# Batch selection in an attention and expert kernel: the first gather ahead of weight rounding, two gate dot products on other engines, score rows of four batches by way of DRAM

## Chip, cores and metric

One core of a Trainium2 chip. The metric is the device time of one execution in microseconds; the kernel before was run three times: 250.52 us median, 248.71 lowest, 251.86 highest. Engines: PE (TensorE), DVE (VectorE), ACT (ScalarE), POOL (GpSimd), SP (SyncE, which here only issues DMAs).

## What is computed

Attention in a sliding window of 64 over 8 batches, 8 heads, 576 positions, head size 64; then, per batch, the 128 rows with the highest gate score go through a two-layer expert and are added back.

```python
scores = scale * q @ k.T; scores = where(0 <= i - j < 64, scores, -1e9)
x = softmax(scores) @ v                      # per batch (576, 512)
s = x @ w_gate                               # gate score of each row
top = argpartition(-s, 128)[:128]            # per batch
out = x
out[top] = x[top] + sigmoid(s[top])[:, None] * (relu(x[top] @ w1) @ w2)   # 512 -> 1024 -> 512
```

All arithmetic that decides is fp32; the expert's operands are split into a rounded high part and a rest, and three products are summed.

## The kernel before

The 72 windows are worked in 36 pairs, called tiles m here (128 rows each; a batch is 4.5 tiles). The main loop at the end of the function has slots n = 0 to 38, and a tile passes through three of them: scores, maxima and exponentials in slot m, transposes of the probabilities in slot m+1, the product with V (av), the normalisation into x and the gate score in slot m+2. The order in which the loop calls the steps is the order of instructions on every engine; each engine works its own list in order. Loads for tile n+2 are issued at the head of slot n on SP, together with one or two 256 KB pieces of the expert weights (the table PIECES) and the stores of finished tiles; pool sizes hold SP back, so that it runs at most some two slots ahead of the engines.

Attention by engine and slot: PE does 32 score matmuls (s), 64 av matmuls and 8 transposes (t). DVE does 8 masked maxima (attn_max, line 270, each followed by a read of its accumulator), a reciprocal, the normalisation (line 322) and the gate (gate_dot, line 230: product with w_gate and sum, 128x512). ACT does 8 exponentials in two halves (line 278), two copies of transposed probabilities (pt) and the sums (z, line 314).

The weight pieces are rounded on POOL (split_w, lines 198 to 203), two instructions each, in the slot after the load: the high part (line 200) and the rest (line 202). Eight pieces are w1 (steps 0 to 7), eight are w2.

A batch is chosen by a generator, choose(b), started in the slot in which the gate scores of its first four tiles are there. It yields the name of the place in the loop at which it wants to go on: R, F, S at the head of a slot, P behind the scores, F0 behind P, R0 behind av, S0, V at the end behind the gate, E behind the expert's share of the slot. Its steps: the gate scores of five tiles, each a column of 128 values, are spread on PE to rows in PSUM, the same on all 128 partitions, by transposes of a broadcast column (spread, line 423), four in one step and the fifth in another; ACT copies them to the tile row (line 430); DVE compares every score with every other (compare, line 439) in steps of two tiles; PE sums the comparisons (lo, line 471); DVE forms the rank and the selection (sel, lines 477 to 487; for most batches the selection is on POOL); PE turns it into row numbers (ix, line 498); DVE makes integers of them (fx, idx, lines 502 and 504); and a DMA on POOL's queue gathers the chosen rows from DRAM (xe, line 506). Batches 0 and 7 are urgent and compare in two parts; batch 0 compares straight from PSUM. For batches 0 and 1 the steps stand at P, R0, S0, F0, for the others at E, R, S, F.

The expert is a second generator (moe). It takes a gathered batch from the slot after its gather on: four transposes of xe (xt, line 528), the split into high part (ACT, line 219) and rest (DVE, line 220), then nine quanta of matmuls at the end of every slot. From slot 12 on it fills PE, and after the last tile it goes on alone.

## Time and profile before

| | |
|---|---|
| median of 3 runs | 250.52 us (248.71 to 251.86) |
| the profiled execution, its own time | 249.5 us |
| its span in the profile | 247.8 us |
| PE busy | 92% |
| DVE busy | 74% |
| ACT busy | 63% |
| POOL busy | 29% |
| mean granted PE clock | 0.991 |

Shares are of the span. The chain of work that ended last runs through the expert's last products and the last scatter; the attention is over at about 190 us, and from there PE works on the expert alone. A share over the whole span is an average over these stages, so the rows below are of single stretches. Busy time of PE includes the overlap of pipelined matmuls. "issue" as the end of an idle time means that the profile shows nothing that was waited for.

### The profile page before, as it was taken

Reading aid. Unit: us, or ns where it says so; the run is one execution under the profiler, and the core shown is the slowest. Engines: PE = TensorE matmul, PEld = TensorE weight load, DVE = VectorE, ACT = ScalarE, POOL = GpSimd, SP = SyncE. Lnnn points to the kernel's source line nnn. Section 1 sums busy time; section 2 is a strip of 40 time slices with the busy share of each in tenths; the row PEclk is TensorE's granted clock in tenths of the full one; section 3 lists DMA queues with packets and bytes.
Section 4 is the critical chain, followed back from the end, with each engine's and each line's share of the span. In section 5 each row is a group of like instructions: output and inputs, shape, how many; then the busy total and the mean of one; then the engine's idle time right before and its main releaser. Section 6 shows DMA issues by size and latency. Waiting matters only on the chain. (4 is left out here: it accounts for less than half of the span.)

```text
span 247.8 us, 10898 instructions
## 1 busy us (share of the span) xinstructions
PE 228.5 (92%) x4406; PEld 198.4 (80%) x4406; DVE 182.5 (74%) x935; ACT 155.4 (63%) x457; POOL 71.1 (29%) x115
## 2 busy tenths in 40 slices
PE   8886787988898999999899999999999899999991
PEld 7675676777787888988788978888888899899891
DVE  0588899778888889879986898798879995342510
ACT  2997876786776986876878768859878122022100
POOL 7406783492640101014016010530061111110011
PEclk9999998899999999999999999999999999999999
DMA  6999998799566766866877672587212221101011
GB/s 231 389 385 376 329 357 263 252 309 356 183 173 177 218 229 194 276 199 188 256 235 236 189 233 91 168 288 246 74 46 87 109 65 44 42 3 42 0 45 42
DMA packets 25154, 47.26 MB, mean 191 GB/s; under 512 B 2960, under 2 KB 3984, under 8 KB 25104
## 3 DMA queue, kind: packets, MB, share of 16 engines
q1 hardware_dynamic: 23680, 42.10, 51.5%
q0 software_dynamic: 1280, 4.20, 5.3%
q8 instruction: 35, 0.57, 1.0%
q10 hardware_dynamic: 144, 0.26, 0.3%
q14 instruction: 15, 0.12, 0.1%
HBM read 35.01 MB, written 11.53 MB: 188 GB/s over the span
## 5 line engine op out<-in xcount | busy, mean ns | idle before, releaser
L278 ACT ACTIVATE p<-p,nm 128x128 f32<-128x128 f32 x288 | 91.8, 394 | 35.4 <-DVE nm L270 33.0
L270 DVE CUSTOM_DVE_ANT_0 p<-s,mask 128x128 f32<-128x128 f32 x288 | 63.5, 285 | 14.8 <-PE s L258 14.7
L304 PE MATMUL av<-v,pt 64*64 64x65 f32 x2176 | 42.1, 220 | 5.8 <-issue 5.8
L304 PEld LDWEIGHTS av<-v,pt 64*64 64x64 f32 x2176 | 39.1, 134 | 7.4 <-issue 6.3
L258 PE MATMUL s<-k,q 64*64 64x128 f32 x1152 | 41.8, 279 | 2.0 <-DVE nm L270 1.0
L286 PE MATMUL t<-ident,p 128*128 128x128 f32 x288 | 41.0, 284 | 0.9 <-DVE fx L502 0.6
L288 ACT COPY pt<-t 128x512 f32<-128x512 f32 x72 | 38.4, 580 | 3.9 <-PE t L286 3.1
L258 PEld LDWEIGHTS s<-k,q 64*64 64x64 f32 x1152 | 32.5, 135 | 10.2 <-issue 8.3
L286 PEld LDWEIGHTS t<-ident,p 128*128 128x128 f32 x288 | 31.5, 142 | 4.7 <-DVE fx L502 1.3
L230 DVE CUSTOM_DVE_ANT_0 jk<-x,wgb 128x512 bf16<-128x512 f32 x36 | 28.7, 797 | 1.2
L666 PE MATMUL yp<-w2h,hh 128*128 128x512 f32 (+1 forms) x72 | 27.8, 386 | 0.0
L322 DVE TENSOR_TENSOR x<-av,z 128x512 f32<-128x512 f32 x36 | 24.9, 692 | 3.4
L676 POOL DMA_INDIRECT out_dram<-xe,idx x8 | 8.1, 1009 | 67.1 <-DVE xe L671 32.4
L666 PE MATMUL yp<-w2l,hh 128*128 128x512 f32 (+1 forms) x72 | 26.9, 374 | 0.0
L666 PE MATMUL yp<-w2h,hl 128*128 128x512 f32 (+1 forms) x72 | 26.9, 373 | 0.0
L270 DVE DVE_READ_ACCUMULATOR2_ANT nm<- 128x1 f32 x288 | 23.6, 82 | 0.0
L439 DVE SCALAR_TENSOR_TENSOR cmp<-row,scores,later 128x128 bf16<-128x128 f32 (+11 forms) x39 | 19.9, 540 | 0.7 <-ACT row L430 0.5
L506 POOL DMA_INDIRECT xe<-out_dram,idx x8 | 8.3, 1040 | 39.9 <-DVE nm L270 29.5
L487 POOL TENSOR_SCALAR sel<-slots,diff 128x128 bf16<-128x128 f32 x16 | 11.7, 741 | 26.8 <-DVE diff L480 26.4
L625 PE MATMUL hp<-xh,w1h 128*128 128x256 f32 x64 | 18.4, 287 | 0.0
L625 PE MATMUL hp<-xl,w1h 128*128 128x256 f32 x64 | 18.2, 285 | 0.0
L625 PE MATMUL hp<-xh,w1l 128*128 128x256 f32 x64 | 18.1, 282 | 0.0
(88 smaller groups left out, 328.2 us busy)
## 6 DMA issues: line engine op xcount, KB each, us to landing
v<-in_v SPq DMA_DIRECT2D x36, 260.0 KB, 5.1
q<-in_q SPq DMA_DIRECT2D x36, 256.0 KB, 4.7
out_dram<-x SPq DMA_DIRECT2D x32, 256.0 KB, 3.9
k<-in_k SPq DMA_DIRECT2D x31, 256.0 KB, 4.8
st<-in_w SPq DMA_DIRECT2D x16, 256.0 KB, 4.1
k<-in_k SPq DMA_DIRECT2D x8, 128.0 KB
out_dram<-x SPq DMA_DIRECT2D x8, 128.0 KB, 2.7
k<-in_k ACTq DMA_DIRECT2D x1, 256.0 KB
```

The lines of the kernel that those rows point to most:

```text
L230: nc.vector.tensor_tensor_reduce(out=junk()[:n, :E], in0=xf[:n], in1=wgb[:n], op0=ALU.mult, op1=ALU.add, scale=1.0, scalar=0.0, accum_out=acc)
L258: nc.tensor.matmul(s[r][c * W:(c + 1) * W, j], Q[m][rs, j, c], keys(m, c, j, rs), start=True, stop=True)
L270: nc.vector.tensor_tensor_reduce(out=pe[:, j, :, r], in0=s[r][:, j], in1=mk, op0=ALU.add, op1=ALU.min, scale=-SCALE, scalar=3.0e38, accum_ ...
L278: nc.scalar.activation(pe[:, j, :, r], pe[:, j, :, r], AF.Exp, bias=nm[:, r, j:j + 1], scale=-1.0)
L286: nc.tensor.transpose(t[:, j, :], pe[:, j, a].rearrange("p r w -> p (r w)"), ident)
L288: nc.scalar.copy(pt, t)
L304: nc.tensor.matmul(av[cs, r, j * D1:(j + 1) * D1], pt[a][rs, j, cs], V[g // 2][rs, g % 2, j], start=a == 0 or o == c, stop=a == 1)
L322: nc.vector.tensor_tensor(out=x.rearrange("p j r d -> p r j d"), in0=av[:, :, :, :D], in1=z[:, 1].unsqueeze(3).to_broadcast([P, 2, NP, D]) ...
L439: nc.vector.scalar_tensor_tensor(out=above[t][r, c0:c1], in0=src[r, c0 - base:c1 - base], scalar=scores[r, m:m + 1], in1=later[r, c0 - a:c ...
L487: (nc.vector if urgent or b in (1, 6) else nc.gpsimd).tensor_scalar(out=sel[r], in0=slots[r], scalar1=diff[r, t:t + 1], scalar2=float(lo - ...
L625: nc.tensor.matmul(hp[:, j], w[:, c, js], a[:, c].rearrange("p u c -> p (u c)"), start=(n == 0), stop=(n == 3 * KC1 - 1))
L666: nc.tensor.matmul(yp[:C, :wide], a[:, c % per, us], w[:, c, es], start=(n == 0), stop=(n == 3 * KC2 - 1))
```

## The change

Six edits.

- Rows through DRAM, for batches 2 to 5: in place of five broadcast transposes, one transpose of the 128x5 block of scores (rt, 5 rows of 128), a small copy on ACT (rs), a DMA of 2.5 KB to a line in DRAM and a second DMA that reads this line to all 128 partitions of the tile row. It starts at P of the slot after the fifth tile's score, and the compares stay in their slots.
- Two gates lent: for tiles 5 and 6 POOL forms the product x * w_gate (prod) and ACT sums it with an accumulating activation, in the next slot. Both run behind other steps of that slot (flush).
- The first gather in front of rounding: the rounding of weight pieces moves from the head of a slot to behind F0, and so behind the first gather on POOL. PIECES loads each piece up to a slot earlier.
- lo of batch 0 moves from P to R0, behind the av matmuls.
- The first row copy of batch 1 and its transposes move to the end of slot 10 and the head of slot 11.
- The subtraction of the first split (batch 0, slot 10) moves behind the next slot's maxima on DVE (EARLY, behind_max).

```diff
 from contextlib import ExitStack
+from functools import partial
 
 import numpy as np
 
@@ -26,6 +27,9 @@
 
 URGENT = (0, 7)
 
+
+BY_DMA = (2, 3, 4, 5)
+
 GROUPS = ((0,), (1,), (2,), (3,), (4, 5), (6, 7))
 
 WARM = 8
@@ -34,7 +38,12 @@
 
 
 
-PIECES = {3: 1, 4: 1, 5: 1, 6: 2, 7: 2, 8: 1} | {n: 2 for n in range(9, 13)}
+PIECES = {2: 1, 3: 1, 4: 1, 5: 2, 6: 1, 7: 1, 8: 2, 9: 2, 10: 2, 11: 2, 12: 1}
+
+
+LENT = (5, 6)
+
+EARLY = 10
 
 CMPS = 2
 
@@ -217,8 +226,17 @@
         for c in range(0, n, step):
             r = slice(c, c + step)
             nc.scalar.copy(hi[:, r], ps[:, r])
-            nc.vector.tensor_tensor(out=lo[:, r], in0=ps[:, r], in1=hi[:, r].bitcast(F32),
-                                    op=ALU.subtract)
+            rest = partial(nc.vector.tensor_tensor, out=lo[:, r], in0=ps[:, r],
+                           in1=hi[:, r].bitcast(F32), op=ALU.subtract)
+            if slot <= EARLY:
+
+                behind_max.append(rest)
+            else:
+                rest()
+
+    behind_max = []
+    behind_exp = []
+    behind_gather = []
 
 
     def junk():
@@ -335,7 +353,19 @@
             nc.sync.dma_start(outs[b + 1][:W, :], xf[W:])
 
     def attn_gate(m):
-        gate_dot(st_x[m], scores[:, m:m + 1])
+        if m not in LENT:
+            gate_dot(st_x[m], scores[:, m:m + 1])
+            return
+        prod = p_h.tile([P, E], F32, tag="h", name=f"prod{m}")
+        behind_gather.append(partial(nc.gpsimd.tensor_tensor, out=prod, in0=st_x[m], in1=wgb,
+                                     op=ALU.mult))
+        behind_gather.append(lambda: behind_exp.append(partial(
+            nc.scalar.activation, junk(), prod, AF.Identity, accum_out=scores[:, m:m + 1])))
+
+    def flush(todo):
+        for op in todo:
+            op()
+        todo.clear()
 
 
 
@@ -358,6 +388,7 @@
         return segs
 
     SEG = [segments(b) for b in range(B)]
+    lines = nc.dram_tensor("lines", (B, NT * P), F32, kind="Internal").ap()
 
     def parts(b):
 
@@ -425,7 +456,7 @@
             if direct:
                 rows[t0 * P] = r_ps
                 return
-            yield "R0" if soon else "R"
+            yield "R0" if soon and t0 else "R"
             c1 = min(end, t1 * P)
             nc.scalar.copy(row[:, t0 * P:c1], r_ps[:, :c1 - t0 * P])
 
@@ -445,10 +476,25 @@
 
         soon = b < 2
         at = "P" if soon else "E"
-        for part, (t0, t1) in enumerate(CUT):
-            yield at
+        if b in BY_DMA:
+            yield "P"
+            while (b, len(CUT) - 1) not in closed or closed[b, len(CUT) - 1] >= slot:
+                yield "P"
+            m0 = segs[0][0]
+            rt = ps_t.tile([P, 512], F32, tag="x", name=f"rt{b}")
+            nc.tensor.transpose(rt[:NT, :P], scores[:, m0:m0 + NT], ident)
+            yield "R0"
+            rs = p_row.tile([P, P], F32, tag="rs", name=f"rs{b}")
+            nc.scalar.copy(rs[:NT], rt[:NT, :P])
+            line = lines[b:b + 1, :]
+            nc.sync.dma_start(line.rearrange("o (t p) -> (o t) p", p=P), rs[:NT])
+            nc.sync.dma_start(row, line.to_broadcast([P, PL]))
+            yield "V"
+        for part, (t0, t1) in enumerate(() if b in BY_DMA else CUT):
+            here = "E" if b == 1 and part == 0 else at
+            yield here
             while (b, part) not in closed or closed[b, part] >= slot:
-                yield at
+                yield here
             yield from spread(t0, t1)
             if urgent:
                 yield "V"
@@ -463,7 +509,7 @@
                 yield "V"
         if b == 1:
             soon, at = False, "E"
-        yield at
+        yield "R0" if b == 0 else at
 
         below = ps_t.tile([P, 512], F32, tag="x", name=f"lo{b}")
         for u in range(NT):
@@ -730,11 +776,6 @@
         for m in range(NM):
             if m + (4 if m < 5 else 3 if m >= NM - 9 else 6) == n:
                 attn_store(m)
-
-        if n in split_at:
-            behind_compares()
-        for st in split_at.get(n, ()):
-            split_w(st)
         step_chain("R")
         step_chain("F")
         step_chain("S")
@@ -744,11 +785,18 @@
             keep_warm(KEEP[n])
         step_chain("P")
         step_chain("F0")
+
+        flush(behind_gather)
+        if n in split_at:
+            behind_compares()
+        for st in split_at.get(n, ()):
+            split_w(st)
         if 0 <= n - 2 < NM:
             attn_pv(n - 2)
         step_chain("R0")
         if n < NM:
             attn_max(n)
+            flush(behind_max)
             attn_exp(n, 0)
         if 0 <= n - 2 < NM:
             attn_sum(n - 2)
@@ -758,6 +806,7 @@
                 attn_transpose(n - 1, a)
         if n < NM:
             attn_exp(n, 1)
+        flush(behind_exp)
         if 0 <= n - 2 < NM:
             attn_out(n - 2)
             attn_gate(n - 2)
```

On POOL, around the first gather (batch 0), slots 8 to 10. st is a loaded weight piece, w1h and w1l its rounded part and rest, xe the gathered rows. Before:

```order
L200 TENSOR_SCALAR w1h<-st_831 128x512
L202 TENSOR_TENSOR w1l<-st_831,w1h 128x512
L200 TENSOR_SCALAR w1h<-st_940 128x512
L202 TENSOR_TENSOR w1l<-st_940,w1h 128x512
L506 DMA xe_1106<-out_dram,idx_1104 128x512
L200 TENSOR_SCALAR w2h<-st_1072 128x512
L202 TENSOR_TENSOR w2l<-st_1072,w2h 128x512
```

and now:

```order
L367 TENSOR_TENSOR prod_930<-x_927,wgb 128x512
L209 TENSOR_SCALAR w1h<-st_835 128x512
L211 TENSOR_TENSOR w1l<-st_835,w1h 128x512
L552 DMA xe_1107<-out_dram,idx_1105 128x512
L367 TENSOR_TENSOR prod_1069<-x_1066,wgb 128x512
L209 TENSOR_SCALAR w1h<-st_941 128x512
L211 TENSOR_TENSOR w1l<-st_941,w1h 128x512
L209 TENSOR_SCALAR w2h<-st_943 128x512
L211 TENSOR_TENSOR w2l<-st_943,w2h 128x512
```

The gather has the last piece of w1 behind it instead of in front, and the two products (prod) stand ahead of the piece of their slot; seven pieces are in front of the gather where there were eight.

On ACT, from the exponentials of slot 9 to those of slot 11; p are probabilities, row the tile of batch 1's scores, xh the high part of batch 0's gathered rows. Before:

```order
L278 ACTIVATE p_1141<-p_1141,nm_1142 128x2x64 x4
L430 COPY row_1180<-r_0_1212 128x512
L278 ACTIVATE p_1251<-p_1251,nm_1252 128x2x64 x4
L314 ACTIVATE z_1265<-av_1217,eps 128x8
L288 COPY pt_0_1272<-t_0_1267 128x512
L288 COPY pt_1_1279<-t_1_1274 128x512
L278 ACTIVATE p_1251<-p_1251,nm_1252 128x2x64 x4
L219 CAST xh_1290<-xt_1292 128x512
L430 COPY row_1180<-r_4_1333 128x128
L278 ACTIVATE p_1361<-p_1361,nm_1362 128x2x64 x4
```

and now:

```order
L296 ACTIVATE p_1148<-p_1148,nm_1149 128x2x64 x4
L367 ACTIVATE jk_1110,scores<-prod_1069 128x512
L296 ACTIVATE p_1253<-p_1253,nm_1254 128x2x64 x4
L332 ACTIVATE z_1267<-av_1220,eps 128x8
L306 COPY pt_0_1274<-t_0_1269 128x512
L306 COPY pt_1_1281<-t_1_1276 128x512
L296 ACTIVATE p_1253<-p_1253,nm_1254 128x2x64 x4
L228 CAST xh_1292<-xt_1294 128x512
L461 COPY row_1188<-r_0_1300 128x512
L461 COPY row_1188<-r_4_1336 128x128
L296 ACTIVATE p_1368<-p_1368,nm_1369 128x2x64 x4
```

The first row copy has left the place ahead of the exponentials of slot 10 and stands behind xh; the sum of the lent gate of tile 6 has come in ahead of slot 10 (that of tile 5 stands likewise at the end of slot 8).

On SP, around the loads that are issued in slots 16 and 17, where batch 2's row is made. Before:

```order
L159 DMA q_1913<-in_q 128x512
L166 DMA k_1915<-in_k 128x512
L174 DMA v_1917<-in_v 128x520
L332 DMA out_dram<-x_1514 128x512
L159 DMA q_2029<-in_q 128x512
L166 DMA k_1915<-in_k 128x512
L174 DMA v_2032<-in_v 128x520
```

and now:

```order
L168 DMA q_1912<-in_q 128x512
L175 DMA k_1914<-in_k 128x512
L183 DMA v_1916<-in_v 128x520
L350 DMA out_dram<-x_1520 128x512
L490 DMA lines<-rs_1972 5x128
L491 DMA row_1785<-lines 128x640
L168 DMA q_2031<-in_q 128x512
L175 DMA k_1914<-in_k 128x512
L183 DMA v_2034<-in_v 128x520
```

Two DMAs stand between the store of one slot and the loads of the next: the first waits for ACT's copy rs, the second for the first.

## Rows read from the trace of the kernel before

**Rows 1.** Busy us by stretch (instructions), then granted clock, DMA share and GB/s

```profile
15.00:20.00 5.00, 4.11 (x148) 3.60 (x136) 4.30 (x21) 4.48 (x15) 1.65 (x2) 1.00 1.05 390
...
40.00:45.00 5.00, 4.88 (x104) 4.22 (x107) 4.74 (x30) 3.29 (x10) 0.49 (x1) 0.67 0.87 286
...
90.00:95.00 5.00, 5.00 (x122) 4.26 (x117) 4.85 (x24) 3.57 (x11) 0.00 (x0) 1.00 0.60 191
...
105.00:110.00 5.00, 5.00 (x101) 4.23 (x97) 4.14 (x24) 4.22 (x14) 0.00 (x0) 1.00 0.82 271
```

**Rows 2.** Timeline of DVE, slots 7 to 9: start us, us, engine, line, operation

```profile
38.38 0.98 DVE L230 CUSTOM_DVE_ANT_0 jk<-x,wgb 128x512 bf16<-128x512 f32 x1
...
39.30 0.27 DVE L439 SCALAR_TENSOR_TENSOR cmp<-r,scores,later 128x64 bf16<-128x64 f32 x1
...
40.32 0.28 DVE L270 CUSTOM_DVE_ANT_0 p<-s,mask 128x128 f32<-128x128 f32 x1
...
44.45 0.69 DVE L230 CUSTOM_DVE_ANT_0 jk<-x,wgb 128x512 bf16<-128x512 f32 x1
...
45.70 0.16 DVE L502 TENSOR_REDUCE fx<-ix 128x1 f32<-128x2 f32 x1 [0.55 <-PE ix L498]
...
45.97 0.28 DVE L270 CUSTOM_DVE_ANT_0 p<-s,mask 128x128 f32<-128x128 f32 x1
```

**Rows 3.** Timeline of PE, slots 8 and 9

```profile
38.50 0.40 PE L471 MATMUL lo<-oneb,cmp 128*128 128x1 bf16 x10
...
39.72 0.98 PE L471 MATMUL lo<-oneb,cmp 128*128 128x1 bf16 x5 [0.82 <-DVE cmp L439]
...
40.63 1.16 PE L304 MATMUL av<-v,pt 64*64 64x65 f32 x64
...
43.62 1.83 PE L258 MATMUL s<-k,q 64*64 64x128 f32 x32
```

**Rows 4.** Timelines of POOL and DVE: a collision in slot 3, the first gather in slot 9

```profile
18.97 1.27 POOL L202 TENSOR_TENSOR w1l<-st,w1h 128x512 fp32r<-128x512 f32 x1
...
18.98 1.81 DVE L230 CUSTOM_DVE_ANT_0 jk<-x,wgb 128x512 bf16<-128x512 f32 x1
...
46.35 1.18 POOL L506 DMA_INDIRECT xe<-out_dram,idx  x1 [5.86 <-DVE nm L270]
```

**Rows 5.** Timelines of ACT, DVE and PE, slots 10 and 11

```profile
50.54 0.59 ACT L430 COPY row<-r 128x512 f32<-128x512 f32 x1
...
55.09 0.69 DVE L220 TENSOR_TENSOR xl<-xt,xh 128x512 fp32r<-128x512 f32 x1 [0.62 <-ACT xh L219]
...
56.58 0.57 PE L304 MATMUL av<-v,pt 64*64 64x65 f32 x19 [0.94 <-issue]
```

**Rows 6.** Timeline of PE, slots 15 to 17: the transposes of batch 2's scores

```profile
82.87 0.60 PE L423 MATMUL r<-ident,scores 128*128 128x128 f32 x4
...
83.40 1.10 PE L258 MATMUL s<-k,q 64*64 64x128 f32 x32
...
88.35 0.27 PE L423 MATMUL r<-ident,scores 128*128 128x128 f32 x1
...
88.55 1.10 PE L258 MATMUL s<-k,q 64*64 64x128 f32 x32
```

**Rows 7.** Timelines of ACT and DVE, slots 20 and 21: batch 3's row copy and compare

```profile
104.31 0.59 ACT L430 COPY row<-r 128x512 f32<-128x512 f32 x1
...
114.50 0.82 DVE L439 SCALAR_TENSOR_TENSOR cmp<-row,scores,later 64x576 bf16<-64x576 f32 x1
```

**Rows 8.** DMA issues: count, KB each, median us to landing; last row: gathers (line 506)

```profile
v<-in_v SPq DMA_DIRECT2D x36, 260.0 KB, 5.1
...
out_dram<-x SPq DMA_DIRECT2D x8, 128.0 KB, 2.7
...
DMA to landing us min/median/max: 3.4/3.7/6.0
```

## The prediction

> **What bounds the kernel now.** I read the busy time in stretches of 5 us first, then the timelines of single engines where two batches' work meet. In the stretches the reader is to see two regimes [rows 1]. From about 60 us on PE is busy for 5.00 of 5 us, with DVE close behind (4.85 in 90 to 95 us, 4.14 in 105 to 110): every slot there carries nine quanta of expert matmuls beside the attention of one pair of windows, and time is gained only by taking work from PE or from what PE waits for. Before that PE has gaps, DVE is at 4.7 of 5 us, and the DMA engines are full (1.05 at 15 to 20 us). The one stretch with a granted clock of 0.67, 40 to 45 us, lies here.
>
> That stretch is the place to look at. Batch 0 is chosen there: its last compares, the counts (lo), the selection (sel, ix) and the index that the first gather needs all go through DVE in between the attention's own work. DVE does the gate of tile 5 at 38.38 us, compares from 39.30, takes the maxima of slot 8 from 40.32, does the gate of tile 6 at 44.45, waits 0.55 us for ix, and starts the maxima of slot 9 at 45.97 [rows 2]. PE does ten of the fifteen lo matmuls at 38.50, then sits 0.82 us for the last compares, and has the slot's 64 av matmuls, which need nothing of that, behind them [rows 3]. Its scores at 43.62 then take 1.83 us, where the same 32 take 1.10 at full clock in row 83.40 [rows 3, 6]: the clock had fallen to the 1.2 GHz level after those gaps.
>
> **The change part by part.**
>
> *Two gates lent.* Tiles 5 and 6 lose their gate on DVE. The first is worth 39.30 - 38.38 = 0.92 us, the second its 0.69 us [rows 2]. In return POOL does one 128x512 product for each; the nearest row is its w1l subtraction of the same size, 1.27 us [rows 4]. POOL waited 5.86 us ahead of the first gather [rows 4], so the first product is covered; without that cover it would hold the gather, by 1.3 us at most, and the transposes of xe stand a slot later. ACT does a 128x512 activation with a sum for each, about the 0.59 us of the row copy at 50.54 [rows 5], at the ends of slots 8 and 9, where it waits for DVE anyway. If ACT were the bound there it would be a loss of up to 1.2 us. Batch 1 needs the score of tile 6 only at the end of slot 10, one slot behind the product.
>
> *lo behind av.* PE does the 64 av matmuls first (1.16 us in the row at 40.63 [rows 3]), and comes to lo when the compares, 0.92 us earlier now, are done. The 0.82 us wait goes; the clock has less reason to fall; ix no longer comes after DVE, so the 0.55 us wait of fx goes too. Sum on DVE up to the maxima of slot 9: 0.92 + 0.69 + 0.55 = 2.16, say 2.1 us earlier. What is late next: scores of slot 9 need the maxima of slot 8, which end 0.92 us earlier, and PE would have them, at full clock, before DVE is ready.
>
> *Gather in front of rounding.* In the trace POOL has no rounding left when the index comes: it idled 5.86 us [rows 4]. By itself this is worth 0. It only keeps the two products and the weight pieces, which are loaded one slot earlier by the new table, from standing in the gather's way. The two pieces of slot 9 now run behind it; they belong to the fourth chunk of the second half of w1 and to w2, first used several slots later, so 0 there as well. The earlier loads fall into a stretch where the DMA engines are full; one piece is 256 KB, at the 390 GB/s of that stretch [rows 1] 0.7 us. Between 0 and -0.7 us; I take 0, because the timeline shows no early engine waiting for q, k or v.
>
> *Subtraction of batch 0 behind the maxima; row copy of batch 1 moved.* In slot 10 the first copy of batch 1's row leaves the place ahead of ACT's exponentials (0.59 us [rows 5]) but an accumulation of about the same length takes its place: 0. DVE waited 0.62 us for ACT and then subtracted for 0.69 us ahead of the maxima of slot 11 [rows 5]; both go behind them, 1.3 us at most. But ACT now has both row copies ahead of the exponentials of slot 11, and PE's gap of 0.94 us in that slot's av [rows 5], for which the profile shows no releaser, stands in nothing that the change touches. I take 0.5 of the 1.3.
>
> Early sum: 2.1 + 0.5 = 2.6 us, between 1.6 (the gates alone) and 2.2 + 1.3 + the gap of 0.9 = 4.4.
>
> *Rows through DRAM.* Four batches lose five transposes each and get one. Four of them cost PE the time from 82.87 to 83.40, 0.53 us, the fifth 88.35 to 88.55, 0.20 us [rows 6]; the new one, of the same 128 columns, again 0.20. So 0.53 us per batch, 2.1 us in all, in a stretch where PE is never idle. All of it is gained if DVE, which still has 0.15 to 0.9 us in 5 free there [rows 1], can follow; none if not. I take all: half a microsecond per four or five slots is well inside that.
>
> The price is a wait. The score row now goes ACT copy, DMA to DRAM, DMA from DRAM to 128 partitions. The second DMA waits on SP for the first, and behind them stand the loads of the next slots, which are issued about two slots ahead and lose only part of that lead. DVE's compares keep their slot. For batch 3 the copy can run about where ACT copied at 104.31; with the scores of that slot in front of it on PE, at about 105.3 to 105.6. The compare that reads it stands at 114.50 [rows 7]: 8.9 us. No DMA in the trace is as small as the first, or reads one DRAM line 128 times like the second. Nearest: 128 KB stores land 2.7 us after issue, loads of v 5.1, gathers up to 6.0 [rows 8]. Twice 2.7 with two issues of about 0.4 is 6.2 us, in time by 2.7; twice 5.1 is 11.0, late by 2.1; twice 6.0 is 12.8, late by 3.9. I take 2.7 for the write (2.5 KB) and about 4 for the row, 7.5 us in all, and a cost of 0, because SP's queue is held while the first lands and the engines have little else in flight.
>
> Sum: 2.6 + 2.1 = 4.7 us. The profiled execution took 249.5 us, 1.0 below the median of the runs; 249.5 - 4.7 = 244.8, so by the median 250.5 - 4.7 = 245.8.
>
> *A rule against it.* At 18.98 us the gate on DVE, 0.69 us elsewhere, took 1.81 us while POOL's subtraction ran from 18.97 for 1.27 us [rows 2, 4]. The Trainium skill (SBUF — State Buffer, "Who interferes with whom") says that a DVE instruction with two SBUF inputs and a GpSimd instruction that reads SBUF exclude each other, and the one that comes first blocks the other for its whole length; this row agrees. By that rule the second product and the pieces behind the gather would hold a later gate by up to about 1.1 us, and the sum would be 3.6 instead of 4.7. The removed gate of tile 5 had itself been stretched to 0.98, so one such collision goes as well. Either way it stays inside the forecast's own range.
>
> **The rivals.**
>
> *The start gives more.* If PE's gap and the fallen clock were both consequences of the traffic and the waits of slots 8 to 11, the early sum goes to 4.4 and the total to 6.5: 244.0. For it: the 1.83 against 1.10 us of scores. Against: "issue" names no releaser.
>
> *The gain is absorbed.* DVE at 4.85 of 5 us takes over as the bound and the transposes buy nothing; the crowded DMA engines cost 0.7 at the start. Left are the two gates, 1.6, less 0.7, up to 1.6: about 249.
>
> *The row is late* (the other side). DVE is in order; a compare that waits for its row holds the maxima of the next slot, then ACT and PE. It decides when copy to landed row takes over 8.9 us. At 5.1 us per DMA it costs 2.1 in each of four batches, 8.4: 250.5 - 4.7 + 8.4 = 254.2. At 6.0 it is 15.6: 261. For it: the landings of v. Against: those were issued into full queues.
>
> *The move does nothing* for the gather: that is my reading already, at 0.
>
> **How the numbers follow.** Forecast 245.8 us, chance 0.42, own range 244 to 248; more at the start 0.27 (242.5 to 244.5); absorbed 0.22 (248 to 250.5); late row 0.09 (250 to 260). Two per cent, about what a measurement of this kernel tells from no change, is 5.0 us: below 245.5 or above 255.5. Faster: 0.27 and 0.19 of the forecast's 0.42, 0.46. Slower: half of the late row, 0.04. Within: 0.50. The range leaves out the lowest tail and the worse part of the late rows: 242.5 to 250.5.
>
> **What would show it.** Right: maxima of slot 9 start about 2 us earlier than 45.97; no wait of PE between lo matmuls and scores of slot 9 at 1.1 us; five transposes of a batch replaced by one with PE still at 5.00 of 5 us; no DVE wait for a DMA at the first compares of batches 2 to 5. Wrong: a DVE idle of over 1 us there; gates stretched beyond 1 us by the products; an early stretch that is no shorter; or PE with idle time between 80 and 160 us, DVE then being the bound.

## The result and the profile after

The changed kernel took 251.9 us (median of 22 runs, 249.76 to 254.35), the kernel before 250.34 (22 runs, 248.57 to 251.86): ratio 1.006, 95% interval 1.0037 to 1.0083. The ratios and intervals, here and below, leave out each kernel's runs that took over 1.5% more than its fastest (here three of the changed kernel's). It is slightly slower; 245.8 had been forecast, and 251.9 lies outside the range. The profiled execution took 250.32 us (span 248.6, mean granted clock 0.997).

The page of the changed kernel, its sums and its DMA row of 40 slices (one digit for 6.2 us, in tenths):

```profile
PE 227.0 (91%) x4390; PEld 195.7 (79%) x4390; DVE 181.1 (73%) x931; ACT 154.3 (62%) x457; POOL 74.3 (30%) x117
...
DMA  6999999897470299289914981995212221001011
```

PE has 1.5 us less work than before (228.5), and still the span is longer: time went into waiting. The DMA row was even before (`6999998799566766866877672587212221101011`); now holes and full slices alternate from slice 11 on.

The stretches that answer to [rows 1], and three where the two kernels differ (same columns):

```profile
40.00:45.00 5.00, 4.06 (x120) 3.24 (x116) 4.18 (x28) 4.31 (x14) 1.96 (x3) 1.00 1.01 335
...
55.00:60.00 5.00, 5.00 (x115) 4.27 (x108) 4.84 (x8) 2.70 (x8) 4.83 (x5) 1.00 0.89 338
...
75.00:80.00 5.00, 4.18 (x97) 3.47 (x97) 3.88 (x20) 3.73 (x12) 0.26 (x1) 1.00 0.02 8
...
90.00:95.00 5.00, 5.00 (x115) 4.27 (x114) 4.85 (x22) 3.13 (x11) 0.60 (x1) 1.00 1.04 397
...
105.00:110.00 5.00, 5.00 (x110) 4.41 (x112) 3.65 (x20) 3.55 (x12) 0.96 (x2) 1.00 0.68 116
...
160.00:165.00 5.00, 4.27 (x110) 3.45 (x109) 4.90 (x25) 2.60 (x9) 1.42 (x3) 1.00 1.07 390
```

The granted clock of 40 to 45 us is now 1.00 where it was 0.67 [rows 1]. At 55 to 60 us DVE is busy for 4.84 us with 8 instructions (before: 4.72 with 23), and POOL for 4.83 beside it (before: 1.27). At 75 to 80 the DMA engines stand still (0.02), at 90 to 95 they are full (1.04); before, the shares were 0.57 and 0.60. At 160 to 165 they are full and PE is busy for only 4.27 of 5 us.

A marker that can be followed through the whole run is the start of each slot's scores on PE:

| scores of slot | 9 | 10 | 11 | 12 | 13 | 15 | 20 | 23 | 31 | 32 | 35 |
|---|---|---|---|---|---|---|---|---|---|---|---|
| before, us | 43.62 | 48.52 | 52.98 | 60.19 | 66.27 | 77.48 | 104.20 | 119.50 | 162.69 | 167.76 | 183.63 |
| after, us | 42.20 | 46.99 | 51.95 | 58.18 | 64.74 | 76.54 | 102.65 | 118.94 | 161.58 | 168.95 | 184.34 |

After is ahead by 1.4 us in slot 9 and by 2.0 in slot 12, keeps 0.6 to 1.6 until slot 31, and loses 2.3 us in that one slot, 1.40 of them in PE's idle times (gaps) at 163.73, 165.61 and 166.39, which are shown below.

**The batch 0 chain** went in part as the prediction said. PE, answering to [rows 3]:

```profile
39.76 0.58 PE L517 MATMUL lo<-oneb,cmp 128*128 128x1 bf16 x15
...
41.62 0.66 PE L304 MATMUL t<-ident,p 128*128 128x128 f32 x4 [0.68 <-DVE diff L526]
42.20 1.10 PE L276 MATMUL s<-k,q 64*64 64x128 f32 x31
```

No wait stands between the lo any more, and the scores take 1.10 us instead of 1.83. But a new wait of 0.68 stands in front of a transpose, and on DVE the wait for ix stayed, 0.61 where 0.55 was to vanish [rows 2]:

```profile
44.13 0.16 DVE L548 TENSOR_REDUCE fx<-ix 128x1 f32<-128x2 f32 x1 [0.61 <-PE ix L544]
```

**The collision in slot 11.** By a collision I mean that a POOL and a DVE instruction run at the same time and take longer than they do alone. POOL's d is a small copy that reads DVE's last compare; it stands ahead of a slot's rounding, so that this does not start before that compare is done. Before the change, DVE and POOL there:

```profile
58.53 0.69 DVE L230 CUSTOM_DVE_ANT_0 jk<-x,wgb 128x512 bf16<-128x512 f32 x1
...
59.24 0.82 DVE L439 SCALAR_TENSOR_TENSOR cmp<-row,scores,later 64x576 bf16<-64x576 f32 x1
...
60.09 0.75 DVE L439 SCALAR_TENSOR_TENSOR cmp<-row,scores,later 128x512 bf16<-128x512 f32 x1
```

```profile
55.02 1.27 POOL L202 TENSOR_TENSOR w2l<-st,w2h 128x512 fp32r<-128x512 f32 x1
60.91 0.19 POOL L402 COPY d<-cnt 128x1 f32<-128x1 f32 x1 [4.62 <-DVE cmp L439]
```

Now DVE first, then POOL:

```profile
54.79 0.69 DVE L367 TENSOR_TENSOR xl<-xt,xh 128x512 fp32r<-128x512 f32 x1
...
56.51 1.69 DVE L248 CUSTOM_DVE_ANT_0 jk<-x,wgb 128x512 bf16<-128x512 f32 x1
...
58.23 1.06 DVE L470 SCALAR_TENSOR_TENSOR cmp<-row,scores,later 64x576 bf16<-64x576 f32 x1
...
59.31 1.66 DVE L470 SCALAR_TENSOR_TENSOR cmp<-row,scores,later 128x512 bf16<-128x512 f32 x1
```

```profile
44.78 1.18 POOL L552 DMA_INDIRECT xe<-out_dram,idx  x1 [2.96 <-DVE nm L288]
45.99 1.28 POOL L367 TENSOR_TENSOR prod<-x,wgb 128x512 f32<-128x512 f32 x1
...
56.36 1.30 POOL L211 TENSOR_TENSOR w2l<-st,w2h 128x512 fp32r<-128x512 f32 x1
57.62 1.06 POOL L209 TENSOR_SCALAR w2h<-st 128x512 fp32r<-128x512 f32 x1
58.76 1.66 POOL L211 TENSOR_TENSOR w2l<-st,w2h 128x512 fp32r<-128x512 f32 x1
61.04 0.18 POOL L433 COPY d<-cnt 128x1 f32<-128x1 f32 x1 [0.62 <-DVE cmp L470]
```

Both engines pay: the subtraction takes 1.66 on POOL where [rows 4] have 1.27, the gate 1.69 on DVE. In the kernel before the same gate and compares took 0.69, 0.82 and 0.75 us: POOL had ended that rounding at 56.29 and then stood for 4.62 us in front of its d. Now it has a product and six pieces behind the gather where it had four pieces, rounds without a pause from 47.2 to 60.4 us, and DVE loses (1.69 + 1.06 + 1.66) - (0.69 + 0.82 + 0.75) = 2.15 us. Slot 11 is not all of it: the first compare of slot 12 takes 1.62 us (at 64.32) where it took 0.60. The next exponentials on ACT, behind the maxima, pay for it:

```profile
61.22 1.28 ACT L296 ACTIVATE p<-p,nm 128x128 f32<-128x128 f32 x4 [3.17 <-DVE nm L288]
```

**The rows.** SP's list, slot 29, and SP's waits (instruction <- what for: us, count, longest):

```profile
152.43 0.28 SPq L490 DMA_DIRECT2D lines<-rs  x1
153.61 0.32 SPq L491 DMA_DIRECT2D row<-lines  x1
153.99 0.42 SPq L168 DMA_DIRECT2D q<-in_q  x1
```

```profile
SPq L490 <- ACT p L296: 20.7, 2, 11.1
SPq L490 <- ACT rs L488: 12.9, 2, 7.0
...
SPq L491 <- DMA lines<-rs: 3.3, 4, 0.8
```

The write lands fast: the row read goes out 1.18 us behind it, and SP waits for it 3.3 us over four batches. What holds SP is the write's own wait for rs: 20.7 + 12.9 = 33.6 us in all four, up to 11.1 at once. Not all of that is new: SP's waits for free buffers behind PE's transposes t fell from 48.4 us before to 12.1. But SP runs ahead of the engines; here it loses its lead, and what it held back goes out in a burst.

**Gaps of PE,** idle times that end in "issue". Later than 65 us the kernel before has none; now there are five, 2.81 us together (0.74 at 115.33, 0.67 at 121.57, and these):

```profile
163.73 0.91 PE L322 MATMUL av<-v,pt 64*64 64x65 f32 x43 [0.71 <-issue]
...
165.61 0.49 PE L304 MATMUL t<-ident,p 128*128 128x128 f32 x3 [0.40 <-issue]
166.39 0.53 PE L304 MATMUL t<-ident,p 128*128 128x128 f32 x3 [0.29 <-issue]
```

The DMA queues of the changed kernel (packets, MB, share) have two of the kind "instruction"; the larger:

```profile
q8 instruction: 35, 0.57, 0.9%
```

That is 16 KB a packet. Set in time beside PE's issue gaps of both kernels, most of these gaps end 1.2 to 1.7 us after such a packet has landed (landed 162.22, gap ends 163.73; landed 113.95, gap ends 115.33; in the kernel before 20.42 and 22.14, 61.57 and 62.89). The gaps at 165.61 and 166.39 have none. In the 18 profiles of this case 113 of the 122 gaps of 0.2 us or more (behind the first such packet) end 1.2 to 1.75 us after one has landed; 35 stretches of 0.55 us are 8% of the span, so this is not chance. The Trainium skill (Runtime: NRT & Kernel Launch, "Instruction fetch mechanics") says that an engine's instructions are refilled in 16 KiB blocks by a DMA queue of its own, and that the cost is mostly hidden. The size of the packets agrees; that the gaps are this fetch is argued from the landing times, and read so, it isn't hidden here.

### The profile page after: what moved, and what is told of

Its sections match the earlier page's. It is cut to its first block, busy times and chain, and to the rows that moved or that the text cites. A ratio compares the mean times of both kernels' runs of the same rounds, so it can differ in the third digit from the quotient of the medians.

```text
span 248.6 us, 10895 instructions
## 1 busy us (share of the span) xinstructions
PE 227.0 (91%) x4390; PEld 195.7 (79%) x4390; DVE 181.1 (73%) x931; ACT 154.3 (62%) x457; POOL 74.3 (30%) x117
## 5 line engine op out<-in xcount | busy, mean ns | idle before, releaser
L322 PE MATMUL av<-v,pt 64*64 64x65 f32 x2176 | 43.4, 221 | 8.4 <-issue 8.2
L322 PEld LDWEIGHTS av<-v,pt 64*64 64x64 f32 x2176 | 39.7, 134 | 11.2 <-issue 9.7
L276 PEld LDWEIGHTS s<-k,q 64*64 64x64 f32 x1152 | 31.9, 133 | 11.0 <-issue 9.8
L304 PEld LDWEIGHTS t<-ident,p 128*128 128x128 f32 x288 | 30.9, 140 | 6.7 <-DVE diff L526 1.6
L248 DVE CUSTOM_DVE_ANT_0 jk<-x,wgb 128x512 bf16<-128x512 f32 x34 | 25.2, 742 | 1.2
L470 DVE SCALAR_TENSOR_TENSOR cmp<-row,scores,later 128x128 bf16<-128x128 f32 (+11 forms) x39 | 22.1, 596 | 0.7 <-ACT row L461 0.5
```

Source lines behind the costliest of these rows:

```text
L248: nc.vector.tensor_tensor_reduce(out=junk()[:n, :E], in0=xf[:n], in1=wgb[:n], op0=ALU.mult, op1=ALU.add, scale=1.0, scalar=0.0, accum_out=acc)
L276: nc.tensor.matmul(s[r][c * W:(c + 1) * W, j], Q[m][rs, j, c], keys(m, c, j, rs), start=True, stop=True)
L304: nc.tensor.transpose(t[:, j, :], pe[:, j, a].rearrange("p r w -> p (r w)"), ident)
L322: nc.tensor.matmul(av[cs, r, j * D1:(j + 1) * D1], pt[a][rs, j, cs], V[g // 2][rs, g % 2, j], start=a == 0 or o == c, stop=a == 1)
L470: nc.vector.scalar_tensor_tensor(out=above[t][r, c0:c1], in0=src[r, c0 - base:c1 - base], scalar=scores[r, m:m + 1], in1=later[r, c0 - a:c ...
```

## The experiments

Two suspects, then, for the loss: POOL's rounding beside DVE (collision), and SP held for the rows (bursts, and with them the gaps). Ratios are to the kernel before on the same chip, with 95% intervals.

**The rows taken out.**

```diff
-BY_DMA = (2, 3, 4, 5)
+BY_DMA = ()
```

> The changed kernel with batches 2 to 5 spread as before (five transposes each), all other edits kept. Theory: SP is held until the small copy of a row is done, the loads of two to three slots are then issued in one burst, and in the bursts PE stands still without a releaser (0.74, 0.67, 0.71, 0.40 and 0.29 us after 110 us, 2.8 us in all). Without the rows those gaps go and the transposes come back (0.9 us): about 250.0 us, 1.9 below the changed kernel, with no PE idle time marked issue after 100 us. Rival, the start alone is to blame (rounding that collides with DVE): 252.8 us, slower than the changed kernel by the transposes.

1.0039 [1.0004, 1.0074]. No issue gap later than 65 us, DMA even; in slot 11 the compares still take 1.06 and 1.67 us. So the gaps come with the rows, and without rows the change is still not faster. Neither the theory's 250.0 us (0.9986) nor the rival's 252.8 (1.0098) was met.

**The row's two DMAs on ACT's queue.**

```diff
-            nc.sync.dma_start(line..., rs[:NT])
-            nc.sync.dma_start(row, line.to_broadcast([P, PL]))
+            nc.scalar.dma_start(line..., rs[:NT])
+            yield "S0"
+            nc.scalar.dma_start(row, line.to_broadcast([P, PL]))
```

> The changed kernel with the two DMAs of a row issued on ACT's queue (the write behind the small copy, the read behind the sums z of the same slot) in place of SP's. Theory (SP held, burst, PE stands still): SP goes on as before, the DMA share after 80 us is as even as in the kernel before, no issue gaps after 100 us, and 249.1 us, 2.8 below the changed kernel. Rival, the rows cost by themselves (the transpose between scores and av, the extra 1.3 MB, the row read from one line): as the changed kernel, 251.9 us.

1.0122 [1.0079, 1.0166]. The gaps are gone; but the wait for the write now holds ACT, once for long. ACT's list:

```profile
108.33 1.07 ACT L306 COPY pt<-t 128x512 f32<-128x512 f32 x2 [1.38 <-DMA lines<-rs]
```

There the DMA engines are 0.99 busy (105 to 108 us), and the read goes out 2.8 us behind the write (105.19 to 107.97), about the 2.7 of the prediction. In the other three batches, at shares of 0.04 to 0.40, it is 1.3 to 1.5 us. PE then waits 1.4 us for the selection on POOL (0.51 and 0.89 in front of ix, up to 115.65). That ACT's wait led to this is not shown, and the rest of the loss is not in these rows. The run says nothing on what the gaps cost: one loss was exchanged for another.

**A pause in the rounding:** no pieces in slot 10, so none is rounded in slot 11.

```diff
-..., 9: 2, 10: 2, 11: 2, 12: 1}
+..., 9: 2, 11: 2, 12: 2, 13: 1}
```

> The changed kernel with no weight piece loaded in slot 10 (two pieces each in slots 11 and 12, one in 13 instead), so that POOL rounds nothing in slot 11. Theory: in slot 11 the gate (1.69 us) and the two compares (1.06 and 1.66) were stretched by POOL's rounding beside them; they go back to 0.69, 0.82 and 0.75, slot 12 starts its maxima 2.1 us earlier, and the time is 249.8 us. Rival, PE is the bound from there on and absorbs it: the three shrink, but the time stays at 251.9 us.

0.9915 [0.9875, 0.9956], better than the theory's 249.8 us (0.998); on another chip (below) 0.9983. DVE of this kernel, slot 11:

```profile
55.42 0.69 DVE L248 CUSTOM_DVE_ANT_0 jk<-x,wgb 128x512 bf16<-128x512 f32 x1
...
56.13 0.82 DVE L470 SCALAR_TENSOR_TENSOR cmp<-row,scores,later 64x576 bf16<-64x576 f32 x1
...
56.97 0.75 DVE L470 SCALAR_TENSOR_TENSOR cmp<-row,scores,later 128x512 bf16<-128x512 f32 x1
```

POOL now waits in front of d, as it did before the change:

```profile
57.80 0.18 POOL L433 COPY d<-cnt 128x1 f32<-128x1 f32 x1 [3.20 <-DVE cmp L470]
```

The scores of slot 13 start at 62.70: 3.6 us ahead of before (66.27), where the change itself is ahead by 1.5. By these two executions the collision took 2.0 us of a start that was worth 3.6. Single executions scatter, though. Slot 13 starts at 65.02 to 66.50 (median 66.06) in the four profiles whose kernel is as before up to there, at 63.69 to 66.00 (65.28) in the four with the changed start and the collision (the change twice, without rows, rows on ACT), and at 62.70 to 64.20 (63.13) in the five with the pause. By the medians the start is worth 2.9 us and the collision takes 2.1 of it. Nor is all of it gone: beyond their bare times, the gates and compares of slots 11 to 13 lose 0.8 us before the change, 3.2 and 3.6 in the change's two profiles, 1.5 and 1.1 in the pause's two. The issue gaps later than 65 us are still there, 2.63 us.

**The rows alone,** put into the kernel before.

```diff
+        if b in BY_DMA:
+            yield "P"
...
+            nc.sync.dma_start(line..., rs[:NT])
+            nc.sync.dma_start(row, line.to_broadcast([P, PL]))
```

> The kernel before with only the rows of batches 2 to 5 by way of DRAM, on SP's queue as in the change. Theory: bursts behind each held row, PE gaps marked issue after 100 us of 2 to 3 us in all, the transposes give 0.9 us back: 252.2 us, slower than before. Rival (the start is to blame, rows are a gain): 249.4 us, faster than before by the transposes.

1.0051 [1.0016, 1.0087]: alone they are a loss, with the DMA row as uneven as after (`6999999898653179559932991799212311101011`), though the profiled execution shows just one gap of 0.57 us.

**The pause, and no rows.** Both edits together.

> The changed kernel without the rows through DRAM and with no weight piece loaded in slot 10. So far, as ratios to the kernel before: changed 1.006, without rows 1.004, with the pause 0.9915, rows alone 1.005. Theory (two independent losses, rows and the collision in slot 11): 0.9915 less 0.002 to 0.005, 0.987 to 0.990, so the fastest yet, and no issue gaps after 100 us. Rival (rows are a gain once the start is right): 0.995, slower than the pause with rows.

0.994 [0.9893, 0.9988]; on another chip (below) 0.9971. No issue gap later than 65 us. It is not the fastest yet, and nearer to the rival's 0.995 than to the theory's 0.990; but its interval overlaps that of the pause with rows.

**The rounding back at the head of its slot.**

```diff
+        if n in split_at:
+            behind_compares()
+        for st in split_at.get(n, ()):
+            split_w(st)
...
-        if n in split_at:
-            behind_compares()
-        for st in split_at.get(n, ()):
-            split_w(st)
```

> The changed kernel with the rounding of weight pieces back at the head of the slot, so that two pieces of slot 9 and the copies that hold POOL until the compares stand where they stood before; everything else kept. Theory (the move behind the gather builds a backlog on POOL, which meets gate and compares of slot 11): the collision goes and the time comes near the pause, 0.992 of the kernel before. Rival (it is the number of pieces and the two products that are too much for POOL, not their place): gate and compares stay stretched, 1.003 to 1.006.

1.0037 [0.9995, 1.008]. Slot 11 is bare, but the gate takes 1.35 us in slot 10 and 1.70 in slot 12: the collision moved by a slot. My theory had expected it to go.

**The two gates given back to DVE.**

```diff
-LENT = (5, 6)
+LENT = ()
```

> The changed kernel with the gates of tiles 5 and 6 back on DVE, everything else kept. Theory: DVE loses the 1.6 us that the two gates cost; POOL has 2.6 us less in front of its rounding, which frees about one compare of slot 11 (0.9 us): 1.008 to 1.01. Rival (the products on POOL are the loss): 1.000 or below.

1.0043 [1.0007, 1.0079]: no different from the change (1.006). POOL still rounds until 60.45, and the compares take 1.06 and 1.66. The two returned gates, of slots 7 and 8, take their bare 0.69; those of slots 10 and 11 are stretched, to 1.59 and 1.12. Both expectations were missed: taking 2.5 us of products from POOL opened no pause.

**A hold of SP alone,** in the kernel before: a 2.5 KB write behind an ACT copy in four slots, its data unused.

```diff
+        if n in (16, 20, 25, 29):
+            nc.scalar.copy(rs[:NT], ident[:NT])
+            nc.sync.dma_start(lines[...], rs[:NT])
```

> The kernel before with nothing but a hold on SP: in slots 16, 20, 25 and 29 ACT copies 5x128 constants behind av, and SP writes them (2.5 KB) to DRAM, where the change writes its row; no row is read back and the scores are spread as before. Theory (the hold makes bursts of loads, in which PE stands still): DMA share swings between near 0 and 1 after 75 us, issue gaps after 100 us of 0.5 to 3 us, 1.004 to 1.009 of the kernel before. Rival (the row read, 320 KB from one line, is what hurts): 1.000.

1.003 [0.9994, 1.0066]. Bursts (DMA row `6999998798562299079835950997212221001011`) and three issue gaps, 1.45 us, of which the longest:

```profile
116.88 0.58 PE L304 MATMUL av<-v,pt 64*64 64x65 f32 x24 [0.79 <-issue]
```

The hold makes the gaps without any row; what it costs in time can't be told from nothing.

**The pause in the kernel before.**

```diff
-PIECES = {3: 1, 4: 1, 5: 1, 6: 2, 7: 2, 8: 1} | {n: 2 for n in range(9, 13)}
+PIECES = {3: 1, 4: 1, 5: 1, 6: 2, 7: 2, 8: 1, 9: 2, 11: 2, 12: 2, 13: 2}
```

> The kernel before with only its load table changed: no weight piece in slot 10, two in slot 13 instead. A control for the pause, which took the changed kernel from 1.006 to 0.9915 of the kernel before. Theory (the pause only takes away the collision in slot 11, which the kernel before does not have: its gate takes 0.69 us there and its compares 0.82 and 0.75): 1.000, within 0.004. Rival (fewer loads in slot 10 help whatever stands there, by a less crowded DMA): 0.990 or below.

1.0084 [1.0052, 1.0117]. The rival that fewer loads in slot 10 help by themselves falls, and so does the theory's 1.000: the table has a cost of its own. The rounding now runs in slot 14 beside a selection on DVE, and PE waits 2.15 us for its ix (at 78.93).

**Full DMA engines without a hold,** in the kernel before: six copies of 256 KB inside DRAM in four slots, unused.

```diff
+        if n in (18, 22, 26, 30):
+            for i in range(6):
+                nc.sync.dma_start(spare[n // 4 - 4, i], w1[i * 64:(i + 1) * 64])
```

> The kernel before with 1.5 MB of copies from DRAM to DRAM (six of 256 KB, part of w1 to an unused tensor) behind the loads of slots 18, 22, 26 and 30; no engine waits for them. Theory (PE stands still without a releaser when the DMA engines are full, whatever fills them): issue gaps of 0.5 us or more in two or more of the four stretches after 75 us, where the kernel before has none, 1 to 4 us in all, and 1.003 to 1.012 of the kernel before. Rival (the gaps come with late operands or with the row itself): no issue gaps after 75 us, 1.000.

0.9985 [0.9939, 1.0031]. The DMA engines are at 0.7 or more from 80 to 173 us, in seven of these fifteen slices at 0.9 (`6999998799664799998899978888212311101011`), and there is no gap later than 69 us. That full DMA engines are enough for the gaps falls; in this part of the run it took the burst behind a hold, and why isn't known.

**The pieces spread, and no rows.**

```diff
-BY_DMA = (2, 3, 4, 5)
-PIECES = {2: 1, 3: 1, 4: 1, 5: 2, 6: 1, 7: 1, 8: 2, 9: 2, 10: 2, 11: 2, 12: 1}
+BY_DMA = ()
+PIECES = {n: 1 for n in range(2, 11)} | {11: 2, 12: 2, 13: 2, 14: 1}
```

> The changed kernel without the rows through DRAM and with one weight piece per slot in slots 2 to 10, two in 11 to 13, one in 14, so that POOL rounds one piece per slot until slot 11. Theory (fewer collisions with the gates of slots 9 to 11, less DMA in slots 5 to 9): gates and compares of slots 10 and 11 within 0.1 us of their bare 0.69, 0.82 and 0.75, and 0.985 to 0.990 of the kernel before, at least as fast as the pause. Rival (the pieces of slots 12 to 15 now collide with the compares of batch 1 and hold the second half of the expert's first layer): 0.995 to 1.005.

0.998 [0.9944, 1.0016], as the rival said. Slot 11 is bare, slot 12 is not (compare 1.63), and in slot 14 the collision takes the selection. DVE, POOL and PE there:

```profile
72.50 2.17 DVE L533 TENSOR_SCALAR sel<-slots,diff 128x128 bf16<-128x128 f32 x4
```

```profile
73.05 1.34 POOL L211 TENSOR_TENSOR w2l<-st,w2h 128x512 fp32r<-128x512 f32 x1
```

```profile
76.86 0.16 PE L544 MATMUL ix<-posb,selh 128*128 128x2 bf16 x1 [2.14 <-ACT pt L306]
```

Where no rounding runs, the four take 0.87 us.

**The pause, with rows that hold no SP:** write on ACT's queue, read on POOL's.

```diff
-            nc.sync.dma_start(line..., rs[:NT])
-            nc.sync.dma_start(row, ...)
+            nc.scalar.dma_start(line..., rs[:NT])
+            nc.gpsimd.dma_start(row, ...)
```

> The changed kernel with the pause of slot 10, and with a row's write issued on ACT's queue and its read on POOL's, so that neither SP nor ACT waits for a landing. Theory (the hold on SP is what the rows cost): DMA share even after 75 us, no issue gaps there, and 0.985 to 0.989 of the kernel before, against 0.9915 with the hold and 0.994 without rows. Rival (the rows cost by the rest): 0.992 to 0.996.

0.9985 [0.9935, 1.0034]. No holes in the DMA row, no gap later than 65 us, and nothing gained on the pause alone. Now POOL's queue is held by its other work: one read goes out only behind a selection, DVE's compare waits 1.42 us for the row (at 139.24), and PE 1.9 us for DVE behind it (at 142.61).

**Four on one chip,** to set the sizes side by side. The change again:

> The changed kernel itself, to stand beside the next three on one chip: 1.006 of the kernel before, 1.003 to 1.009. Issue gaps after 100 us again, 1 to 3 us in all, since SP is held.

1.0088 [1.0054, 1.0123]. The gaps came out smaller than expected: one after 100 us, 0.86 us. The collision is as large, but does not meet the same instructions: gate 0.73, compares 1.06 and 1.67 in slot 11, and the gate of slot 12 takes 1.74.

The same with each piece of slots 10 to 12 rounded a slot later and loaded as in the change:

```diff
-            split_at.setdefault(n + 1, []).append(loaded)
+            split_at.setdefault(n + (2 if n >= 10 else 1), []).append(loaded)
```

> The changed kernel with every load as it is, but the pieces loaded from slot 10 on rounded a slot later, so that POOL rounds nothing in slot 11. Theory (the collision of the rounding with gate and compares is the loss): gate 0.69, compares 0.82 and 0.75 in slot 11, and as the pause, 0.990 to 0.997. Rival (the pause helped by taking loads out of slot 10): the three are short, but the time stays at 1.003 to 1.009.

1.0005 [0.9965, 1.0046]; the gate and the compares of slot 11 take 0.69, 0.82 and 0.75. The time lies between what theory and rival gave. The pause again:

> The changed kernel with the pause of slot 10, a second time. Theory: 0.988 to 0.996, at least 0.007 below the changed kernel on this chip. Rival (the first result was a lucky chip): 0.998 to 1.003.

0.9983 [0.9941, 1.0025]: well below the change, but in the rival's range, so the 0.9915 of the first chip was in part luck. The pause without rows again:

> The pause without rows through DRAM, a second time. Theory (rows cost 0.002 to 0.005 by the hold on SP): 0.002 to 0.005 below the pause with rows on this chip. Rival (the saved transposes outweigh the hold once the collision is gone): 0.002 or more above it.

0.9971 [0.9929, 1.0013]. Neither interval of the two kernels with the same rows and slot 11 bare (1.0005, 0.9983) touches that of the change: by the ratios the collision costs 0.8 to 1.05%, 2.1 to 2.6 us, against 2.15 in the trace. Its size is less sure than its presence: the medians of all 12 runs of each are 251.1 us (the change), 250.2, 249.7 and 249.0, and 248.95 for the kernel before, so 0.9 and 1.5 us for the collision. The rows are not told from nothing here (0.9983 against 0.9971).

**What the gaps cost** can be read from the profiles of these runs. The lead on the kernel before at the scores of slot 20 (104.20 us there) and at the end of the span (247.8), with the gaps after 100 us:

| profile | gaps, us | lead at slot 20, us | lead at the end, us | won or lost, us |
|---|---|---|---|---|
| the pause again | 3.00 | 2.87 | -0.18 | -3.1 |
| the change | 2.81 | 1.55 | -0.82 | -2.4 |
| the pause | 2.63 | 4.04 | 2.14 | -1.9 |
| gates given back | 1.58 | 1.46 | -0.08 | -1.5 |
| hold of SP alone | 1.45 | -0.23 | -1.72 | -1.5 |
| the change again | 0.86 | 0.29 | 0.30 | 0.0 |
| rows alone | 0.57 | 1.03 | 1.39 | +0.4 |
| pause without rows, twice | none | 2.49, 1.09 | 2.83, 1.62 | +0.3, +0.5 |
| rows taken out | none | -1.24 | -0.56 | +0.7 |
| copies inside DRAM | none | 0.14 | 0.72 | +0.6 |
| pieces spread, and the pause on before | none | -0.74, -1.63 | -0.20, -1.02 | +0.5, +0.6 |

The more gaps, the more is lost, somewhat over a microsecond for each microsecond of gaps; where nothing holds SP and the rows are spread on PE, nothing is lost. (Rows on ACT's queue, and rows that hold no SP, have no gaps and lose 1.8 and 0.6 us, where the waits named above stand; two profiled executions of 252 us and more are left out.) How many gaps the hold brings differs from execution to execution, 0.57 to 3.00 us, and the ratios average over that.

## Why the prediction was wrong

**The step that failed** is "the two pieces of slot 9 now run behind it ... so 0 there as well". It asked when the weights are needed, which is late enough, and not what POOL would then run beside. Gather and products in front pushed these pieces, and those of slot 10 behind them, into POOL's pause: the 4.62 us in slot 11 in which DVE did gate and compares undisturbed. "A rule against it" named the mechanism, but at one collision of 1.1 us in one gate; it was one gate and two compares, 2.15 us in the trace and 2.1 to 2.6 by the ratios on one chip. That the rounding in slot 11 is the cause is shown: taken out of it, by the loads or by the order alone, gate and compares are bare and the ratio falls. This is what the Trainium skill (SBUF — State Buffer, "Who interferes with whom") says of DVE instructions with two SBUF inputs beside GpSimd, and the rows of slot 11 agree: the compare at 59.31 and the subtraction at 58.76 take 1.66 us each, alone 0.75 and 1.27.

**The start** was sized about right: 2.6 forecast (1.6 to 4.4), 2.9 us by slot 13 once the collision is out (2.1 to 3.6 in single profiles). The parts were not all what I took them for. The gather came 1.57 us earlier (46.35 to 44.78), not 2.1, because the 0.55 us wait for ix stayed; and this pair flatters it. Over the five profiles with the old start and the ten with the new one and the same place of the rounding, the medians are 46.4 and 45.7, and the wait for ix is up to 2.22 us. The clock and the scores' 1.10 us came as said, as a rule: between 40 and 50 us the granted clock of a 5 us stretch falls below 0.9 in four of the five profiles with the old start and in three of thirteen with a new one. The scatter of single executions may come in part from there. xl lost its wait by moving. The gates lent are not seen in the time (1.0043 without them, 1.006 with); that the collision takes what DVE wins is my reading.

**The rows: "0.53 us per batch, 2.1 us in all"** was mis-sized. A transpose's price is what it adds to the step between its neighbours. The steps on PE, first the kernel before, around [rows 6], then the changed kernel:

```profile
82.64 0.40 PE L666 MATMUL yp<-w2h,hh 128*128 128x512 f32 x1
...
84.33 1.11 PE L304 MATMUL av<-v,pt 64*64 64x65 f32 x64
...
88.12 0.39 PE L666 MATMUL yp<-w2l,hh 128*128 128x512 f32 x1
```

```profile
81.68 0.40 PE L712 MATMUL yp<-w2h,hh 128*128 128x512 f32 x1
82.01 1.10 PE L276 MATMUL s<-k,q 64*64 64x128 f32 x32
83.04 0.27 PE L485 MATMUL rt<-ident,scores 128*5 128x128 f32 x1
83.25 0.97 PE L322 MATMUL av<-v,pt 64*64 64x65 f32 x49
```

From yp straight to s it is 82.01 - 81.68 = 0.33 us. With four r between them it was 83.40 - 82.64 = 0.76, with one 88.55 - 88.12 = 0.43: so the five cost 0.43 + 0.10 = 0.53, not 0.73. The new one costs 83.25 - 82.01 = 1.24 against 0.93 from s straight to av (83.40 [rows 6] to 84.33 in the kernel before), 0.31, not 0.20. The net is 0.22 per batch, 0.9 in all. A reason for part of the steps is in the Trainium skill (TensorEngine Tiling (Array Packing), "Key Properties"): a change of tiling mode drains TensorE. The old transposes stood where 128x128 work changed to 64x64 anyway; the new one stands between two kinds of 64x64 work and brings two changes. The trace has the steps, but no run here separates the drain.

**The hold of SP, put at "a cost of 0"** because the loads behind it "lose only part of that lead", failed in a way I had not thought of. No compare waited for its row, and the late row didn't come, as forecast; the write even took 1.2 us instead of 2.7, because the held queue had drained. But the holds were 33.6 us and not four landings of 1.2: I had looked at the wait of the second DMA for the first, and not at the first's wait for ACT. The lead turned into bursts, and in the profile PE lost 2.8 us to gaps, more than the 0.9 won. That the hold makes the gaps is shown (with it: the change, the pause, the rows alone, the hold alone; without it none later than 69 us), and so is what they cost, by the table above. That they are a fetch of instructions is argued from landing times, and why a burst brings them is open. What the rows cost in the median is not settled: alone 0.5%, but not told from nothing on top of the pause; the gaps of one execution can be 0.57 us or 3.00.

**The sum.** From the profiled 249.5 of before: less 3.6 (start), plus 2.0 (collision), less 0.9 (rows), plus 2.8 (gaps) is 249.8; the profile has 250.3. This explains the two profiled executions, 0.8 us apart; the medians are 1.6 apart. By size alone 251.9 lies among the rivals in the range of "the row is late" (250 to 260, chance 0.09), but no compare waited for its row. Two signs of being wrong did come, each by another cause: gates stretched beyond 1 us, by the rounding and not by the products, and idle time of PE between 80 and 160 us, without DVE as the bound. The best versions found are the change with the pause, with or without rows: 0.9915 and 0.9983, 0.994 and 0.9971, on average about half a per cent faster than before, and on the chip of the last four not told from it. By the sum with a start of 2.9, the pause without rows should have been at 249.5 - 2.9 = 246.6; its two profiled executions took 246.67 and 247.89. They are ahead by 3.1 and 2.1 us in slot 13 and by 2.8 and 1.6 at the end, so what the start wins is kept. Why its runs as a whole show less (1.5 and 0.7 us by the ratios) stays open.

## What to carry to other kernels

Before work is moved off one engine's way, look at what it will stand beside in its new place, slot by slot: an idle stretch of POOL may be what keeps DVE at full speed. A wait put on the queue that issues the loads takes the lead from the loads behind it, and its length is set by the producer, not by the DMA. A start marker of one profile against one of another can be off by 2 us: compare several. Price a small matmul by the step between its neighbours with and without it, not by its own row.

## What the runs showed of the hardware that was not expected

- POOL's rounding and DVE's two-input instructions stretch each other by up to 2.7 times: gate 0.69 to 1.69, compares 0.75 to 1.66 and 0.60 to 1.62, and on POOL 0.62 to 1.06 and 1.27 to 1.66. DVE's selection, with one array as input, does it too: four in 2.17 us instead of 0.87.
- PE's idle times with no releaser go mostly with 16 KB packets of the instruction queue, ending 1.2 to 1.75 us after the landing (113 of 122 in 18 profiles). They come early in the run and behind a hold of SP, and after 69 us not under DMA engines kept at 0.7 to 0.9 by copies.
- A 2.5 KB write let the DMA that waits for it go out after 1.2 us in all four rows of the change, where the DMA engines were idle (share 0.01 to 0.06), and once, at a share of 0.99, after 2.8.
- Runs of one kernel scatter with the mean granted clock, which is not the same in each: the kernel without rows took 249.3 us at 0.996 and 251.35 at 0.988. On the one chip where both were run side by side, the change had 0.990 in the median and the kernel before 0.989; so the clock didn't make the change slower, and differences of under half a per cent can hardly be told here.
